# All of the program in the scheduler's table: keys, loads and weight conversion included, with other tile sizes, ranks and engine shares

## The chip, the cores and the metric

The kernel runs on one core of one Trainium2 chip. The metric is the device time of one launch, in microseconds (us), from the runs' own clock; a profile of one execution stands beside it.

## The reference, cut to what matters

Agent attention over 12480 tokens of width 128, and two feed-forward layers of width 2048 on its output, one after the other:

```python
def sm(a, b):
    s = scale * (a @ b.transpose(0, 2, 1))
    s = s - s.max(-1, keepdims=True)
    e = np.exp(s)
    return e / (e.sum(-1, keepdims=True) + 1e-09)
agent_v = sm(agents, k) @ v            # 49 agents over all keys
x = sm(q, agents) @ agent_v            # each token over 49 agents
h = x @ w_in                           # layer 1
P = a[0] + a[1]*h + a[2]*h**2 + a[3]*h**3
Q = 1.0 + abs(b[0])*abs(h) + abs(b[1])*h**2
x = (P / (Q + 1e-6)) @ w_out
r = np.maximum(x @ w2_in, 0.0)         # layer 2
out = (s * (r * r) + b) @ w2_out
```

All arrays are float32 except the four weight matrices. These come as float64, as pairs of 32-bit words, and the kernel makes float32 of them itself.

## The kernel before, in words

**Keys first.** The softmax over the keys needs all keys, so the kernel starts with 13 blocks of keys and values (`BLOCKS`: 12 of 1024 rows, one of 192). For a block `load_kv` loads keys and values on the SP queue, `keys_scores` (PE) multiplies agents and keys, `keys_max` (DVE) takes the running maximum, `keys_exp` (ACT) the exponentials, `keys_trans` and `keys_av` (PE) multiply them with the values, `keys_sum` and `keys_acc` (DVE) carry sum and product over to the next block. `keys_fold` closes it, and a copy into `avt` (L539) is its last step. The order of this stage is written out by hand in a loop at the end of the kernel.

**Weights.** Each of the four matrices is converted in 4 pieces (`CONV`, numbers 0 to 15: `w_in`, `w_out`, `w2_in`, `w2_out`). One piece is a load, two ACT passes (`conv_act`), four DVE passes (`conv_bit`: L390, L391, L393, L395) and a product and a sum on POOL (`conv_pool`: L407, L409). Pieces 0 to 9, and most of 10, stand between the steps of the key blocks in the same loop; the others come later, from the scheduler. Pieces of `w2_in` are also split into a high and a low part (`conv_hi`, `conv_lo`).

**The product of the agents' values and `w_in`** (`avw_mm`, `avw_hi`, `avw_lo`) is formed after `avt`, so that layer 1 of a token tile needs only its 49 softmax weights.

**Token tiles.** `TILES` cuts the tokens in 24 tiles of 512 and one of 192. A tile is worked on in units, 8 for a tile of 512: a unit is 1024 columns of hidden values. Layer 1 of unit p is the chain: `m1_h` on PE (L681, four matmuls), `m1_z` and `m1_abs` on ACT, `m1_u2` and `m1_u3` on DVE (L702, L705), `m1_w` on POOL (L696, L698), `m1_ln` and `m1_exp` on ACT, `m1_e`, `m1_m` and `m1_g` on DVE (L717, L721, L732), `m1_out` on PE (L740). The PSUM buffer that `m1_h` writes has one bank that all units share (`mid`), so `m1_h` of the next unit waits for `m1_u3` of this one. In the units of `ADD_POOL` the step `m1_g` isn't done by DVE but as two steps on POOL, `m1_a` (L725) and `m1_ga` (L729). After the last unit of a tile `m1_hi` and `m1_lo` (L751, writes `xl`) hand its result to layer 2: `m2_h` on PE (L763 to L765, into the one bank `bb`), `m2_relu` on ACT, the square on ACT or on POOL (L774, by `SQ_ACT`), `m2_out` on PE (L778). Layer 2 runs about one tile behind layer 1, so that both fill the same stretch of time.

**What sets the order.** `main_jobs` lists the steps of everything behind the keys with an engine, an estimated duration, predecessors, the buffers they use and a rank (unit number plus `RANK` of their kind). `in_order` places them one by one: the engine that can start first takes the job of lowest rank among those that are ready. `SLOTS` says how many buffers a kind has. The result is one fixed order on each engine:

```python
soon = max(free[e], min(at[k] for k in ks)) + 1e-9 + PATIENCE[e]
k = min((k for k in ks if at[k] <= soon), key=lambda k: jobs[k]["rank"])
```

Every engine works through its list in this order; a step that waits holds up all that stand behind it. All big transfers are issued on SP's queue. L326 is the one line that issues every ACT operation.

## Time and profile before

| | |
|---|---|
| time, median of 3 runs | 1355.6 us (1351.86 to 1356.43) |
| the profiled execution's own time | 1355.32 us |
| its span, first to last instruction | 1353.5 us |
| PE busy | 1259.5 us (93%) |
| DVE busy | 1228.9 us (91%) |
| ACT busy | 1178.3 us (87%) |
| POOL busy | 1122.5 us (83%) |
| mean granted PE clock | 0.974 |

The shares are means over stages with very different limits: a start in which no engine is full, some 1100 us in which tiles follow each other with the same pattern, and an end. The span leaves out 1.8 us of the execution's time.

### The profile page before, as it was taken

The numbers are of one execution on the slowest core, as the hardware profiler recorded it, in microseconds if no ns is written. First come the engines' busy times: TensorE is split into PE (matmuls) and PEld (weight loads), VectorE is DVE, ScalarE is ACT, GpSimd is POOL, SyncE is SP. The second block draws the span as 40 slices with busy tenths as digits, with TensorE's granted clock in tenths as the row PEclk, the third lists the DMA queues.
The fourth block names the chain that finished last, engine by engine and source line by source line (L and its number), as shares of the span: only waits on it lengthen the run. The fifth ranks groups of instructions, "written<-read, shape, count | busy, mean of one in ns | idle before, by whom it ended". The sixth has DMA issues, their size and how long they took to land.

```text
span 1353.5 us, 12969 instructions
## 1 busy us (share of the span) xinstructions
PE 1259.5 (93%) x4213; PEld 718.9 (53%) x4213; DVE 1228.9 (91%) x1178; ACT 1178.3 (87%) x1524; POOL 1122.5 (83%) x701
## 2 busy tenths in 40 slices
PE   5565699999999999999999999999999999999998
PEld 3342355555555555555555555555555555555565
DVE  5879989999999999999999999999999999999980
...
DMA packets 14005, 34.81 MB, mean 26 GB/s; under 512 B 2193, under 2 KB 2673, under 8 KB 13937
## 3 DMA queue, kind: packets, MB, share of 16 engines
...
q10 hardware_dynamic: 576, 0.00, 0.0%
...
## 4 chain that ended last, share of the span: by engine, by line
PE 61%; DVE 14%; POOL 11%; ACT 9%; issue 4%; DMA 1%; SPq 0%; ACTq 0%; DVEq 0%; POOLq 0%
PE acc L740 19%; PE acc L778 15%; PE xb L681 9%; PE bb L763 5%; PE bb L764 5%; PE bb L765 5%; POOL w_all L698 4%; POOL g_all L729 4%; DVE z_all L702 4%; DVE u_all L705 3%; ACT t_all L326 3%; POOL w_all L696 2%; DVE g_all L717 2%; ACT v_all L326 2%; DVE rb L721 2%
## 5 line engine op out<-in xcount | busy, mean ns | idle before, releaser
L698 POOL TENSOR_TENSOR w_all<-w_all,t_all 128x1024 f32<-128x1024 f32 (+1 forms) x196 | 464.3, 2369 | 18.6 <-ACT w_all L326 2.5
L740 PE MATMUL acc<-g_all,wout_sb 128*128 128x512 f32 (+1 forms) x800 | 374.2, 600 | 23.5 <-POOL g_all L729 11.8
L778 PE MATMUL acc<-v_all,w2out_sb 128*128 128x512 f32 (+1 forms) x800 | 379.3, 582 | 0.2 <-ACT o L326 0.2
L696 POOL TENSOR_SCALAR w_all<-t_all,absb 128x1024 f32<-128x1024 f32 (+1 forms) x193 | 232.4, 1204 | 111.1 <-ACT t_all L326 111.0
L326 ACT ACTIVATE v_all<-bb 128x512 f32<-128x512 f32 (+1 forms) x392 | 235.2, 600 | 45.8 <-PE bb L765 37.6
L702 DVE TENSOR_TENSOR z_all<-xb,z_all 128x1024 f32<-128x1024 f32 (+1 forms) x196 | 238.4, 1216 | 37.6 <-ACT z_all L326 35.8
L763 PE MATMUL bb<-xh,w2l 128*128 128x512 f32 (+1 forms) x400 | 251.6, 629 | 8.4 <-ACT v_all L326 7.7
L705 DVE SCALAR_TENSOR_TENSOR u_all<-z_all,prm,xb 128x1024 f32<-128x1024 f32 (+1 forms) x196 | 249.9, 1275 | 9.9
L326 ACT ACTIVATE t_all<-xb 128x1024 f32<-128x1024 f32 (+1 forms) x196 | 200.1, 1021 | 59.8 <-PE xb L681 59.1
L740 PEld LDWEIGHTS acc<-g_all,wout_sb 128*128 128x128 f32 x800 | 148.2, 193 | 181.2 <-issue 113.6
L717 DVE SCALAR_TENSOR_TENSOR g_all<-w_all,rb 128x1024 f32<-128x1024 f32 (+1 forms) x196 | 236.9, 1209 | 2.6 <-ACT rb L326 2.6
L326 ACT ACTIVATE z_all<-xb,prm 128x1024 f32<-128x1024 f32 (+1 forms) x196 | 236.6, 1207 | 0.0
L326 ACT ACTIVATE l_all<-w_all 128x1024 f32<-128x1024 f32 (+1 forms) x196 | 205.9, 1065 | 9.0 <-POOL w_all L698 7.1
L326 ACT ACTIVATE rb<-l_all 128x1024 f32<-128x1024 f32 (+1 forms) x196 | 204.3, 1042 | 3.5 <-DVE g_all L732 3.5
L774 POOL TENSOR_TENSOR v_all<-v_all 128x1024 f32<-128x1024 f32 x96 | 182.3, 1899 | 22.9 <-ACT v_all L326 22.9
L732 DVE SCALAR_TENSOR_TENSOR g_all<-u_all,prm,rb 128x1024 f32<-128x1024 f32 (+1 forms) x151 | 192.3, 1274 | 5.2
L778 PEld LDWEIGHTS acc<-v_all,w2out_sb 128*128 128x128 f32 x800 | 149.4, 189 | 78.2 <-issue 55.7
L721 DVE SCALAR_TENSOR_TENSOR rb<-g_all,rb 128x1024 f32<-128x1024 f32 (+1 forms) x151 | 184.2, 1220 | 3.5
L681 PE MATMUL xb<-pt,avwh 128*128 128x512 f32 (+1 forms) x400 | 167.7, 421 | 20.9 <-DVE u_all L705 15.5
L681 PE MATMUL xb<-pt,avwl 128*128 128x512 f32 (+1 forms) x400 | 157.9, 396 | 0.0
L764 PE MATMUL bb<-xh,w2h 128*128 128x512 f32 (+1 forms) x400 | 156.7, 392 | 0.0
L765 PE MATMUL bb<-xl,w2h 128*128 128x512 f32 (+1 forms) x400 | 155.4, 388 | 0.0
...
## 6 DMA issues: line engine op xcount, KB each, us to landing
...
```

Source lines behind the costliest of these rows:

```text
L326: return nc.scalar.activation(out=out, in_=in_, func=func, **kw)
L681: on_banks(nc.tensor.matmul(out=dst, lhsT=w[:, c * P:(c + 1) * P], rhs=pts[OF_UNIT[p][0]], start=first, stop=not first), {x}, "pe")
L696: nc.gpsimd.tensor_scalar(out=w, in0=t, scalar1=absb[:, 1:2], scalar2=absb[:, 0:1], op0=ALU.mult, op1=ALU.add)
L698: nc.gpsimd.tensor_tensor(out=w, in0=w, in1=t, op=ALU.mult)
L702: on_banks(nc.vector.tensor_tensor(out=z, in0=h_view(p), in1=z, op=ALU.mult), banks(p), "dve")
L705: on_banks(nc.vector.scalar_tensor_tensor(out=view("u", p), in0=view("z", p), scalar=a1, in1=h_view(p), op0=ALU.add, op1=ALU.mult), banks( ...
L717: nc.vector.scalar_tensor_tensor(out=view("g", p), in0=view("w", p), scalar=C1, in1=r_view(p), op0=ALU.add, op1=ALU.mult)
L740: nc.tensor.matmul(out=acc1[i][:, :n], lhsT=wout_sb[:, c * D:(c + 1) * D], rhs=g[:, at_(p, k), o:o + n], start=(c == 0), stop=(c == NCH - 1))
L763: nc.tensor.matmul(out=dst, lhsT=w2l[:, ws], rhs=xh, start=True, stop=False)
L764: nc.tensor.matmul(out=dst, lhsT=w2h[:, ws], rhs=xh, start=False, stop=False)
L765: nc.tensor.matmul(out=dst, lhsT=w2h[:, ws], rhs=xl, start=False, stop=True)
L778: nc.tensor.matmul(out=accs[1][:, :n], lhsT=w2out_sb[:, c * D:(c + 1) * D], rhs=m2_view(p)[:, k, o:o + n], start=(c == 0), stop=(c == NCH ...
```

## The change

What it does, part by part:

- **Tiles**: the first has 256 tokens (4 units) and the last 448 (8 units), with 23 of 512 between them. There are 196 units as before.
- **Order of the start**: key blocks, their loads, the conversion, the agent softmax of the first tile and the constants' loads become jobs of `start_jobs`, and `in_order` orders them with all others. The hand-written loop is gone. Loads of pieces 4 and up follow the last key block's load. Key blocks have 7 buffer pairs (in `l_all`, `g_all`, `u_all`) where they had 4.
- **Fewer operations on DVE in a key block**: the running maximum and its scaling are one TENSOR_SCALAR (before TENSOR_TENSOR and TENSOR_SCALAR); the running sum is a TENSOR_SCALAR (before SCALAR_TENSOR_TENSOR).
- **Conversion**: `conv_pool` becomes `conv_mul` (POOL) and `conv_add`, on DVE for pieces 0 to 9 and on POOL for the others; the clamp of pieces 4 to 15 goes from DVE to POOL.
- **Shares**: `ADD_POOL` has 3 units in 8 (before 2), `SQ_ACT` 5 in 8 (before 4), `W_ACT` units 4 to 11.
- **Buffers**: `z`, `t` 3 (before 2), `v` 5 (before 3).
- **Ranks** and planner constants are all others.
- Three matmuls on zeros stand ahead of the first key block; the four small constants are loaded on SP's queue and no more on ACT's.

```diff
-TILES = [512] * 24 + [192]
+TILES = [256] + [512] * 23 + [448]
...
-ADD_POOL = {p for p in range(12, NU - 4) if p % 8 in (1, 5)}
-SQ_ACT = {p for p, (_, j) in enumerate(OF_UNIT) if j in (0, 2, 4, 6) or p > NU - 5}
+W_ACT = {4, 5, 6, 7, 8, 9, 10, 11}
+ADD_POOL = {p for p in range(12, NU - 4) if p % 8 in (1, 4, 6)}
+SQ_ACT = {p for p, (_, j) in enumerate(OF_UNIT) if j in (1, 2, 4, 5, 7) or p > NU - 5}
...
+RANK = dict(h=-4.37, z=-5.75, abs=-0.66, y=-4.61, w=-1.15, u2=-4.49, u3=1.0, ln=7.57, exp=4.25, e=4.12,
...
+KV_TAG = "lgu"
...
+def start_jobs(add):
+
+    for i in range(2):
+        add(("load_q", i), "sp", 0.65, -58 + 30 * i, "key", (), [("qt", i)], -400)
+    last = NB - 1
+    for t, n in enumerate(BLOCKS):
+        o, at, part = KEY * t - 60, t - 300, n / 1024
+        kv = [(KV_TAG[t % 3], "kv", t, y) for y in range(2)]
...
+        add(("load_kv", t), "sp", 2.65 * part, o - AHEAD * KEY, "key", (), kv, at)
+        add(("keys_scores", t), "pe", 1.02, o, "key", [("load_kv", t)], kv + [sp], at)
+        add(("keys_max", t), "dve", 0.9, o, "key", [("keys_scores", t)] + prior, [sp], at)
...
+        add(("conv_load", n), "sp", 1.35, o - 8, "conv", [("load_kv", NB - 1)] if n >= 4 else [], raw, at)
...
+            clamp = n >= CLAMP and k == 0
+            add(("conv_bit", n, k), *(("pool", 0.65) if clamp else ("dve", us)), o, "conv",
+                [("conv_bit", n, k - 1) if k else ("conv_act", n)], raw + cv + tmp, at, True)
+        add(("conv_mul", n), "pool", 1.28, o, "conv", [("conv_bit", n, 3)], raw + cv + tmp, at)
+        add(("conv_add", n), *(("dve", 0.6) if n < DVE_ADDS else ("pool", 1.28)), o, "conv",
+            [("conv_mul", n)], raw + cv + tmp, at, True)
...
         if t:
-            nc.vector.tensor_tensor(out=m, in0=m, in1=cf[:, 0:1] if t == NB - 1 else ms[t - 1],
-                                    op=ALU.max)
-        nc.vector.tensor_scalar(out=nms[t], in0=m, scalar1=-SCALE, scalar2=None, op0=ALU.mult)
+            nc.vector.tensor_scalar(out=nms[t], in0=m, scalar1=-SCALE, op0=ALU.mult, op1=ALU.min,
+                                    scalar2=cf[:, 0:1] if t == NB - 1 else nms[t - 1])
+        else:
+            nc.vector.tensor_scalar(out=nms[t], in0=m, scalar1=-SCALE, scalar2=None, op0=ALU.mult)
...
-            nc.vector.scalar_tensor_tensor(out=ssum, in0=ssum, scalar=fs[t], in1=rss.pop(t),
-                                           op0=ALU.mult, op1=ALU.add)
+            nc.vector.tensor_scalar(out=ssum, in0=ssum, scalar1=fs[t], scalar2=rss.pop(t), op0=ALU.mult,
+                                    op1=ALU.add)
...
+        nc.vector.memset(win_sb[:, :512], 0.0)
...
+        for _ in range(3):
+            nc.tensor.matmul(out=bb_, lhsT=win_sb[:, :P], rhs=win_sb[:, :512], start=True, stop=True)
...
-        conv_load(0)
-        load_q(0)
-        load_kv(2)
-        conv_load(1)
-        load_q(1)
-        keys_scores(0)
...
```

**The loads at the start.** SP's queue, from the first load on. Before (`l_all` and `g_all` hold key blocks, `v_all` and `z_all` raw words of weights, `qt` queries, `agp` the agents):

```order
L812 DMA agp<-in_agents_dram 128x49
L448 DMA l_all<-in_k_dram 128x1024
L450 DMA l_all<-in_v_dram 128x1024
L448 DMA g_all<-in_k_dram 128x1024
L450 DMA g_all<-in_v_dram 128x1024
L372 DMA v_all<-in_moe_w_in_dram 128x1024
L594 DMA qt_131<-in_q_dram 128x512
L448 DMA l_all<-in_k_dram 128x1024
L450 DMA l_all<-in_v_dram 128x1024
L372 DMA z_all<-in_moe_w_in_dram 128x1024
```

And with the change, the same place (`u_all` holds key blocks too):

```order
L502 DMA l_all<-in_k_dram 128x1024
L504 DMA agp<-in_agents_dram 128x49
L506 DMA l_all<-in_v_dram 128x1024
L502 DMA g_all<-in_k_dram 128x1024
L506 DMA g_all<-in_v_dram 128x1024
L659 DMA qt_131<-in_q_dram 128x256
L502 DMA u_all<-in_k_dram 128x1024
L506 DMA u_all<-in_v_dram 128x1024
L502 DMA l_all<-in_k_dram 128x1024
L506 DMA l_all<-in_v_dram 128x1024
L424 DMA v_all<-in_moe_w_in_dram 128x1024
```

Four key blocks now stand ahead of the first piece of weights, where two stood.

**DVE after the keys.** Before, from the copy into `avt` to the first unit of layer 1 (`avwl` is the low part of the agents' product with `w_in`):

```order
L539 COPY avt<-bb 128x128
L390 TENSOR_SCALAR w_all<-w_all 128x512
L391 TENSOR_SCALAR w_all<-w_all 128x512
L393 SCALAR_TENSOR_TENSOR w_all<-v_all,w_all 128x512
L553 SCALAR_TENSOR_TENSOR avwl<-acc_79,cf,avwh 128x256
L553 SCALAR_TENSOR_TENSOR avwl<-acc_78,cf,avwh 128x256
L395 TENSOR_SCALAR t_all<-w_all 128x512
L617 TENSOR_REDUCE mx_657<-ss_102 128x4
L553 SCALAR_TENSOR_TENSOR avwl<-rb,cf,avwh 128x512 x2
L553 SCALAR_TENSOR_TENSOR avwl<-acc_79,cf,avwh 128x512
L702 TENSOR_TENSOR z_all<-xb,z_all 128x1024
```

With the change (L467 is `conv_add`, L449, L451 and L453 are conversion, L619 is `avw_lo`), the same place in part:

```order
L605 COPY avt<-bb 128x128
L467 TENSOR_TENSOR wout_sb<-u_all 128x512
L467 TENSOR_TENSOR wout_sb<-w_all 128x512
L619 SCALAR_TENSOR_TENSOR avwl<-acc_79,cf,avwh 128x256
L619 SCALAR_TENSOR_TENSOR avwl<-acc_78,cf,avwh 128x256
L453 TENSOR_SCALAR t_all<-w_all 128x512
L449 TENSOR_SCALAR w_all<-w_all 128x512
L682 TENSOR_REDUCE mx_623<-ss_102 128x4
L451 SCALAR_TENSOR_TENSOR w_all<-v_all,w_all 128x512
L467 TENSOR_TENSOR wout_sb<-u_all 128x512
```

Conversion that stood among the key blocks now stands here. From behind the copy into `avt` to the second L816 (`xl` of the second tile) the changed list has 30 operations of conversion, 15 each of `m1_u2` and `m1_u3`, and 13, 12 and 12 of `m1_e`, `m1_m` and `m1_g`. The list before, from the same copy to the second L751, has 24 of conversion, 19 each of `m1_u2` and `m1_u3`, and 17, 17 and 15 of the other three.

**DVE in a steady tile.** Before, around the hand-over to layer 2 (L702, L705 are `m1_u2`, `m1_u3`; L717, L721, L732 are `m1_e`, `m1_m`, `m1_g`; L617 is of the agent softmax):

```order
L702 TENSOR_TENSOR z_all<-xb,z_all 128x1024
L705 SCALAR_TENSOR_TENSOR u_all<-z_all,prm,xb 128x1024
L717 SCALAR_TENSOR_TENSOR g_all<-w_all,rb 128x1024
L751 TENSOR_TENSOR xl_3487<-acc_78,xh_3475 128x512
L721 SCALAR_TENSOR_TENSOR rb<-g_all,rb 128x1024
L732 SCALAR_TENSOR_TENSOR g_all<-u_all,prm,rb 128x1024
L702 TENSOR_TENSOR z_all<-xb,z_all 128x1024
```

With the change, the same place (L767, L770, L782, L786, L797 are the same five steps):

```order
L767 TENSOR_TENSOR z_all<-xb,z_all 128x1024
L770 SCALAR_TENSOR_TENSOR u_all<-z_all,prm,xb 128x1024
L782 SCALAR_TENSOR_TENSOR g_all<-w_all,rb 128x1024
L816 TENSOR_TENSOR xl_3685<-acc_78,xh_3677 128x512
L786 SCALAR_TENSOR_TENSOR g_all<-g_all,rb 128x1024
L767 TENSOR_TENSOR z_all<-xb,z_all 128x1024
L770 SCALAR_TENSOR_TENSOR u_all<-z_all,prm,xb 128x1024
```

The fifth step, `m1_g`, is missing in the interval that holds the hand-over. In a whole tile three of the eight intervals between one `m1_u2` and the next lack it, and two of these hold the hand-over and the `mx` row. Before, two lack it; one of them holds the `mx` row, and the hand-over stands in an interval of all five steps.

## Rows read from the trace of the kernel before

**Rows 1.** Windows: length, busy PE, PEld, DVE, ACT, POOL, clock, DMA, GB/s

```profile
10.00:75.20 65.20, 42.86 (x317) 25.40 (x315) 49.27 (x112) 32.79 (x78) 25.78 (x23) 0.86 0.75 286
75.20:162.90 87.70, 52.29 (x123) 28.59 (x124) 76.75 (x86) 57.83 (x73) 69.34 (x49) 0.73 0.09 27
162.90:217.30 54.40, 50.52 (x159) 28.84 (x158) 49.27 (x42) 48.46 (x61) 40.15 (x23) 0.97 0.01 2
266.30:315.70 49.40, 48.64 (x157) 27.62 (x157) 47.40 (x44) 46.12 (x59) 44.53 (x27) 1.00 0.03 11
```

**Rows 2.** Timeline of DVE: start, length, line, out<-in; stage ends

```profile
74.88 0.28 DVE L539 COPY avt<-bb 128x128 f32<-128x128 f32 x1
...
162.86 0.69 DVE L751 TENSOR_TENSOR xl<-acc,xh 128x512 fp32r<-128x512 f32 x1 [0.92 <-ACT xh L326]
...
217.29 0.68 DVE L751 TENSOR_TENSOR xl<-acc,xh 128x512 fp32r<-128x512 f32 x1
...
1301.96 0.69 DVE L751 TENSOR_TENSOR xl<-acc,xh 128x512 fp32r<-128x512 f32 x1
```

**Rows 3.** Timeline of PE and DVE inside one steady tile

```profile
622.00 1.02 PE L778 MATMUL acc<-v_all,w2out_sb 128*128 128x512 f32 x2
...
622.85 0.50 PE L763 MATMUL bb<-xh,w2l 128*128 128x512 f32 x1
...
633.28 1.22 DVE L702 TENSOR_TENSOR z_all<-xb,z_all 128x1024 f32<-128x1024 f32 x1
...
639.52 1.22 DVE L702 TENSOR_TENSOR z_all<-xb,z_all 128x1024 f32<-128x1024 f32 x1
...
642.28 0.47 PE L681 MATMUL xb<-pt,avwh 128*128 128x512 f32 x1 [0.18 <-DVE u_all L705]
...
645.23 1.23 DVE L702 TENSOR_TENSOR z_all<-xb,z_all 128x1024 f32<-128x1024 f32 x1 [0.70 <-ACT z_all L326]
...
648.18 0.39 PE L681 MATMUL xb<-pt,avwh 128*128 128x512 f32 x1
...
649.10 0.60 PE L658 MATMUL bb<-ident,pp 128*128 128x128 f32 x4
```

**Rows 4.** Windows of the keys' loads; last column GB/s

```profile
0.00:10.00 10.00, 1.66 (x4) 0.32 (x4) 1.79 (x6) 1.49 (x2) 2.15 (x11) 1.00 0.49 179
30.00:40.00 10.00, 5.36 (x50) 2.91 (x48) 9.51 (x20) 5.05 (x13) 5.23 (x5) 1.00 1.03 408
```

**Rows 5.** Timeline of PE, scores of the last full key block

```profile
62.62 1.08 PE L459 MATMUL xb<-g_all,agp 128*64 128x512 f32 x4
```

**Rows 6.** Groups of DVE instructions, first 75.2 us: count | busy, mean ns

```profile
L511 DVE SCALAR_TENSOR_TENSOR ssum<-ssum,f,rs 128x1 f32<-128x1 f32 x12 | 10.8, 904 | 1.0 <-ACT f L326 1.0
```

**Rows 7.** Timeline, DVE beside POOL

```profile
23.68 1.28 POOL L409 TENSOR_TENSOR win_sb<-w_all 128x512 f32<-128x512 f32 x1
...
23.71 1.25 DVE L511 SCALAR_TENSOR_TENSOR ssum<-ssum,f,rs 128x1 f32<-128x1 f32 x1
...
75.05 1.27 POOL L407 TENSOR_TENSOR u_all<-u_all,t_all 128x512 f32<-128x512 f32 x1 [2.45 <-DVE t_all L395]
...
75.08 1.51 DVE L390 TENSOR_SCALAR w_all<-w_all 128x512 f32<-128x512 f32 x1
```

**Rows 8.** Groups of DVE instructions, 100 to 163 us

```profile
L393 DVE SCALAR_TENSOR_TENSOR win_sb<-v_all,win_sb 128x512 int32<-128x512 int32 x3 | 4.5, 1499 | 0.0
...
L395 DVE TENSOR_SCALAR v_all<-win_sb 128x512 int32<-128x512 int32 x3 | 1.4, 465 | 0.0
```

**Rows 9.** Groups of POOL and ACT instructions, 600 to 800 us

```profile
L725 POOL TENSOR_SCALAR u_all<-u_all,one,prm 128x1024 f32<-128x1024 f32 x8 | 9.7, 1208 | 0.0
...
L729 POOL TENSOR_TENSOR g_all<-g_all,u_all 128x1024 f32<-128x1024 f32 x9 | 21.6, 2395 | 0.0
...
L774 POOL TENSOR_TENSOR v_all<-v_all 128x1024 f32<-128x1024 f32 x16 | 30.4, 1900 | 0.0
...
L326 ACT ACTIVATE v_all<-v_all 128x1024 f32<-128x1024 f32 x16 | 17.2, 1074 | 0.0
```

More of the change, by code (lines that the diff above doesn't have):

```diff
@@ L97, in add @@
         n = len(jobs)
+        if engine == "pe":
+            us *= slowed(key, unit)
         jobs[key] = dict(engine=engine, us=us, rank=(unit + RANK[kind], n), after=list(after),
@@ L177, in main_jobs @@
             if p in ADD_POOL:
-                add(("m1_a", p), "pool", w * 0.00117 + 0.07, p, "a", [("m1_u3", p)], [u])
+                add(("m1_a", p), "pool", w * 0.00117, p, "a", [("m1_u3", p)], [u])
                 add(("m1_ga", p), "pool", w * 0.00233, p, "ga", [("m1_m", p), ("m1_a", p)], [g, u])
@@ L183, in main_jobs @@
                 prior = [("m1_out", p, 0)] if k else [("m1_out", p - 1, 1)] if j else []
+                cs = range(0 if i else (2 * j + k + 1) * cpb)
                 add(("m1_out", p, k), "pe", pe_us(4, w / 2, cpb), p + 1, "out",
-                    [("m1_ga" if p in ADD_POOL else "m1_g", p)] + prior,
-                    [g, ("acc0", i)])
+                    [("m1_ga" if p in ADD_POOL else "m1_g", p)] + prior
+                    + [("conv_add", 4 + c // 4) for c in cs], [g, ("acc0", i)])
         end = f + UNITS[i] - 1
@@ L206, in main_jobs @@
                 add(("m2_out", p, k), "pe", pe_us(4, w / 2, cpb), behind, "m2out",
-                    [sq] + [("conv_pool", 12 + c // 4) for c in cs] + prior, [v, ("acc1", i)])
+                    [sq] + [("conv_add", 12 + c // 4) for c in cs] + prior, [v, ("acc1", i)])
             behind += 1
@@ L252, in in_order @@
         order.append(key)
-        slow = 1.5 if engine == "pe" and start < COLD else 1
+        slow = 1
         free[engine] = end = start + slow * jobs[key]["us"]
@@ L397, in conv_dve, with conv_mul, conv_add @@
         ]
-    def conv_bits(n):
-        for op in conv_dve(n):
-            op()
-    def conv_pool(n):
+    def conv_mul(n):
+        _, lf, s = cvs[n]
+        nc.gpsimd.tensor_tensor(out=lf, in0=lf, in1=s, op=ALU.mult)
+    def conv_add(n):
         name, _, u = CONV[n]
-        b, lf, s = cvs[n]
+        b, lf, _ = cvs[n]
         sl = slice(u * CW, (u + 1) * CW)
-        nc.gpsimd.tensor_tensor(out=lf, in0=lf, in1=s, op=ALU.mult)
         dst = {"in": win_sb, "out": wout_sb, "2out": w2out_sb}.get(name)
-        nc.gpsimd.tensor_tensor(out=b if dst is None else dst[:, sl], in0=lf, in1=b, op=ALU.add)
+        engine = nc.vector if n < DVE_ADDS else nc.gpsimd
+        engine.tensor_tensor(out=b if dst is None else dst[:, sl], in0=lf, in1=b, op=ALU.add)
     def conv_bit(n, k):
```

294 lines of the change are left out of this document (128 added, 166 removed).

## Prediction

> **What bounds the kernel now.** I read the windows of each stage first. The reader is to see four stages that are limited by different things [rows 1]. From 10 to 75 us, the keys, PE is busy 43 of 65 us and DVE 49. From 75 to 163 us, the first tile of layer 1, PE is busy 52 of 88 us at a granted clock of 0.73, so its work there is worth less than it looks; DVE is busy 77. From 163 us on PE is nearly full, and in a steady tile it is busy 48.6 of 49.4 us, DVE 47.4, ACT 46.1, POOL 44.5. The timeline of DVE dates the borders: the copy into `avt` ends at 75.2 us, `xl` of the first tile starts at 162.9, of the second at 217.3, of the twenty-fourth at 1302.0, which makes 49.3 us for a tile [rows 2].
>
> In the steady tile PE looks like the bound, but is not quite. Its own work, from the distance between starts, is 0.85 us for a matmul of an output (622.00 to 622.85) [rows 3], 0.92 for the four of `m1_h` (648.18 to 649.10) [rows 3], so 0.69 for the three of `m2_h`, and 0.6 for the transposes; with 0.9 for the agent scores, 32 x 0.85 + 8 x 0.92 + 16 x 0.69 + 1.5 = 47.1 us. So 2.2 us of each tile are waits. DVE sets them, together with one chain: from one `m1_u2` to the next DVE takes 6.24 us with all five steps (633.28 to 639.52). Where `m1_g` is POOL's, four steps would take 5.0, but the next `m1_u2` comes after 5.71 (639.52 to 645.23), the last 0.70 waiting for `m1_z`: `m1_u2` and `m1_u3` release the shared bank, PE fills it (642.28, after a wait), ACT reads it twice, DVE goes on [rows 3]. Six intervals of five steps, two of that chain, and about 1.0 for the hand-over and the agent softmax: 6 x 6.24 + 2 x 5.71 + 1.0 = 49.9, against 49.3 measured. The account is 0.5 too high, but says where the time is.
>
> **The keys' stage.** The change lets loads run ahead: seven buffer pairs, and only four pieces of weights ahead of the last key block. Twelve full blocks are 12.6 MB, the four pieces 2.1, queries 0.4: 15.1 MB. The first 10 us moved 1.8 MB (179 GB/s), full streaming is 408 GB/s [rows 4], so the last lands at 10 + 13.3/0.408 = 43 us. Then the closing chain: from the scores of the last full block at 62.62 [rows 5] to the end of the copy at 75.2 [rows 2] it took 12.5 us. I take `avt` at 43 + 12.5 = 55 us. DVE is not later: it had 49.3 us of work there [rows 1], and loses up to 12 x (0.9 - 0.2) = 8 us if the running sum, at 904 ns for one column [rows 6], no longer waits, and a quarter of the conversion. Bounds: 50 if the closing chain shrinks to 7 with conversion out of its way; 62 if POOL's products hold DVE as before. The three matmuls on zeros and the constants' loads on SP cost nothing: PE has no keys yet, and the small loads stand among block loads of 2.6 us each (1.05 MB at 408 GB/s).
>
> **POOL beside DVE.** The running sum that started 0.03 us after a POOL product of 1.28 us took 1.25 us; but a TENSOR_SCALAR of 512 columns that started 0.03 us after one of 1.27 took 1.51 [rows 7]. So the new form may wait as well; a row for one column beside POOL there is not. I give the new form no gain of its own, since the loads are later. The sum that `conv_add` makes on DVE has no row either; the nearest with two inputs in SBUF is L393, at 1.5 us each in the second stage, against 0.47 for L395 [rows 8].
> The Trainium skill, page "SBUF — State Buffer", section "Who interferes with whom", says that VectorE with two SBUF inputs or in a two-port mode, which it lists for tensor_scalar, and GpSimd exclude each other for a whole instruction. By that rule the new running sum would gain nothing and the five sums behind `avt` would wait; the trace agrees for the forms it has, 1.25 and 1.51 us.
>
> **From `avt` to the second tile's `xl`.** DVE's work decides: 76.75 + 49.27 = 126.0 us busy in 87.7 + 54.4 = 142.1 [rows 1], 89%. The changed list has 8 fewer of `m1_u2` and `m1_u3`, and 4, 5 and 3 fewer of `m1_e`, `m1_m`, `m1_g`: 20 at a fifth of 6.24 are 25.0 us less. It has 6 more of conversion, at 0.47 to 1.5; I take 0.6, since few of them are of the waiting kind, so 3.6 more. That leaves 104.6 us, at the same 89% 118. `xl` of the second tile: 55 + 118 = 173 us. Bounds: 50 + 104.6/0.95 = 160, and 62 + 124 = 186, with the six and the five sums at 1.5.
> At this point 12 units of layer 1 are done, before it was 16 at 217.3. Four units more at the steady 49.3/8 are 24.6: 198 against 217, **19 us gained**. Behind it PE has layer 2 of the short tile and layer 1 of the next to do; it isn't full there, and needn't be, since DVE sets the pace.
>
> **The steady tiles.** `m1_g` leaves DVE in a third interval, where the chain takes over; the hand-over and the `mx` row now lie in intervals that waited anyway. 5 x 6.24 + 3 x 5.71 + 0.4 = 48.7 against 49.9: 1.1 us less for a tile. The other engines get closer to it: ACT one more square of 1.07, so 47.2; POOL one more addition and product less one square, 44.5 + 1.21 + 2.40 - 1.90 = 46.2 [rows 1, 9]. At a tile of 48.2 us ACT would be 98% busy, and what it does in order (`m1_z` and `m1_abs` behind squares and logarithms) will come late now and then. I take 0.8 us. Bounds: 0, if that eats all, and 1.3; PE's own 47.1 allows no more than 2.2. From the sixteenth unit on there are 180 units, 22.5 tiles: **18 us gained**.
>
> **The end.** Behind the last `m1_out` the list before has 9 `m2_h` and 14 `m2_out` of 512 columns and 8 of each of 384; the changed one 16 of each of 448 and 4 `m2_out` of 512. At 0.69 and 0.85 that is 27.4 and 25.0 us: **2 us gained**, give or take 2.
>
> **Sum.** 1353.5 - 19 - 18 - 2 = 1314.5 of span; with the 1.8 us around it 1316.3 for an execution like the profiled one, whose 1355.3 is the median of the runs (1355.6) but for 0.3. I say 1316.
>
> **The rivals.**
> *The steady tile stays at 49.3.* For it: ACT and POOL have lists of 47.2 and 46.2 us and no slack to absorb each other. Against: every engine still has 2 us a tile left. 1316 + 18 = 1334.
> *The stalls only move.* The running sum keeps its 0.7 us in 12 blocks and the five DVE sums cost 0.9 more each: 8 + 4.5, 1328. For it: both waiting forms [rows 7]. Against: in the keys' stage the loads are later. This is also what the rule of the Trainium skill's page "SBUF — State Buffer" (section "Who interferes with whom") gives.
> *The keys' stage is bound otherwise*, by PE at its lower clock (mean 0.86 there now [rows 1]) or by buffers that come free late: `avt` at 70, 1331.
> *All of it goes better*: `avt` at 50, DVE 95% busy behind it, 1.3 us a tile: 1316 - 5 - 8 - 11 = 1292.
> *Slower.* POOL's list puts a `m1_a` or `m1_ga` directly ahead of `m1_w`. If each of the three additions a tile delays `m1_w` by its 1.21 us, the logarithm waits, in ACT's order the relu behind it waits, and with the one bank `bb` PE: 3.6 us against the 2.2 of waits there are, so 1.4 a tile more, 22.5 x 1.4 = 32, less 21 of start and end: 1355 + 11 = 1366. It decides from 21/22.5 = 0.93 us a tile on, a tile of 50.2. Against it: `t` has three buffers, so POOL may run late by a unit.
>
> **How the numbers follow.** Forecast 0.52, with 1303 to 1327 as its own range from the bounds of its terms; steady tile unchanged 0.18; stalls move 0.10; better 0.10; keys otherwise 0.05; slower 0.05. From 1296 to 1338 leaves out about 0.06 below and 0.10 above. Under 0.3%, 4 us, a difference can't be told from none here. All cases but the last lie over 4 us below 1355.6: faster 0.93, same 0.02, slower 0.05.
>
> **What would show it.** The copy into `avt` at 50 to 60 us, with loads at some 400 GB/s until about 43; `xl` of the second tile at 165 to 181; starts of `xl` 48.2 to 48.9 apart from then on, DVE busy 46 to 47 of it, ACT near 47; intervals of four steps on DVE at 5.7 with the hand-over inside. The prediction fails if `xl`s are 49.3 or more apart, or if DVE, behind `avt`, waits for POOL's `m1_w` or for conversion.

## The result, and the profile after

The changed kernel takes 1336.4 us (median of 4 runs, 1334.5 to 1338.2) where the kernel before takes 1354.0 beside it: a ratio of 0.987, 95% interval 0.984 to 0.990. The time lies inside the range of the prediction (1296 to 1338), but the gain is 17.6 us where 39.6 were forecast (1355.6 to 1316).

The windows of the changed kernel by stage, in the columns of [rows 1]:

```profile
10.00:66.26 56.26, 38.01 (x305) 23.76 (x303) 35.10 (x89) 29.77 (x74) 19.10 (x15) 0.80 0.76 286
66.26:83.74 17.48, 10.02 (x30) 6.52 (x30) 13.14 (x20) 9.63 (x17) 13.75 (x10) 0.70 0.39 136
83.74:171.49 87.75, 57.41 (x202) 40.43 (x202) 78.97 (x80) 69.06 (x82) 74.79 (x49) 0.73 0.06 18
188.41:240.79 52.38, 47.84 (x147) 27.80 (x146) 46.19 (x42) 47.06 (x60) 45.47 (x28) 0.92 0.03 8
581.54:630.21 48.67, 48.54 (x158) 27.29 (x157) 46.10 (x42) 47.23 (x60) 46.34 (x29) 1.00 0.04 11
```

The borders, from the timeline of DVE (the copy into `avt`, the first and the thirteenth `m1_u2`, `xl` of the first, second, third and last full tile):

```profile
65.98 0.28 DVE L605 COPY avt<-bb 128x128 f32<-128x128 f32 x1
83.74 1.21 DVE L767 TENSOR_TENSOR z_all<-xb,z_all 128x1024 f32<-128x1024 f32 x1
137.69 0.41 DVE L816 TENSOR_TENSOR xl<-acc,xh 128x256 fp32r<-128x256 f32 x1
171.49 1.23 DVE L767 TENSOR_TENSOR z_all<-xb,z_all 128x1024 f32<-128x1024 f32 x1
188.41 0.69 DVE L816 TENSOR_TENSOR xl<-acc,xh 128x512 fp32r<-128x512 f32 x1 [0.92 <-ACT xh L383]
240.79 0.69 DVE L816 TENSOR_TENSOR xl<-acc,xh 128x512 fp32r<-128x512 f32 x1
1263.31 0.68 DVE L816 TENSOR_TENSOR xl<-acc,xh 128x512 fp32r<-128x512 f32 x1
```

These rows are to be laid beside [rows 1, 2] by units done, since the tiles are cut differently. At 240.8 us the changed kernel has done 20 units. The kernel before has 16 at 217.3 and 24 at 266.3, so 20 at 241.8: **the whole start has gained 1.0 us**. At 1263.3 it has done 188, the kernel before at 1277.9 (midway between its last two full tiles): 14.6, so the steady tiles gained 13.6. The spans end 17.1 apart (1353.5 and 1336.4), so the end gained 2.5. Steady tile and end came nearly as forecast (18, of 22.5 tiles where these are 21, and 2); of the 19 us of the start one came.

Two further profiles of the same kernel (below) have `avt` at 64.1 and 64.4 and the third `xl` at 238.8 and 239.5, so the start's gain is 1 to 3 us, whichever profile is taken.

### The profile page after: what moved, and what is told of

Its sections match the earlier page's. It is cut to its first block, busy times and chain, and to the rows that moved or that the text cites. A ratio compares the mean times of both kernels' runs of the same rounds, so it can differ in the third digit from the quotient of the medians.

```text
span 1336.4 us, 13092 instructions
## 1 busy us (share of the span) xinstructions
PE 1262.7 (94%) x4219; PEld 719.7 (54%) x4219; DVE 1193.9 (89%) x1142; ACT 1209.0 (90%) x1552; POOL 1168.4 (87%) x721
## 4 chain that ended last, share of the span: by engine, by line
PE 72%; ACT 17%; DVE 4%; issue 3%; DMA 2%; POOL 1%; SPq 0%; ACTq 0%; DVEq 0%
PE acc L805 21%; PE acc L843 17%; PE xb L746 10%; PE bb L828 8%; PE bb L829 6%; PE bb L830 6%; ACT z_all L383 4%; ACT v_all L383 3%; ACT l_all L383 3%; ACT t_all L383 3%; PE bb L665 2%; ACT rb L383 2%; ACT xh L383 1%; PE acc L565 1%; DMA g_all<-in_k_dram 1%
## 5 line engine op out<-in xcount | busy, mean ns | idle before, releaser
L805 PE MATMUL acc<-g_all,wout_sb 128*128 128x512 f32 (+2 forms) x800 | 387.4, 598 | 13.8 <-DVE g_all L797 13.8
L843 PE MATMUL acc<-v_all,w2out_sb 128*128 128x512 f32 (+2 forms) x800 | 375.8, 581 | 0.1
L767 DVE TENSOR_TENSOR z_all<-xb,z_all 128x1024 f32<-128x1024 f32 (+1 forms) x196 | 238.2, 1215 | 50.0 <-ACT t_all L383 49.9
L770 DVE SCALAR_TENSOR_TENSOR u_all<-z_all,prm,xb 128x1024 f32<-128x1024 f32 (+1 forms) x196 | 249.7, 1274 | 5.9
L782 DVE SCALAR_TENSOR_TENSOR g_all<-w_all,rb 128x1024 f32<-128x1024 f32 (+1 forms) x196 | 237.2, 1210 | 7.1 <-ACT rb L383 3.2
L805 PEld LDWEIGHTS acc<-g_all,wout_sb 128*128 128x128 f32 x800 | 152.9, 196 | 123.2 <-issue 68.8
L828 PE MATMUL bb<-xh,w2l 128*128 128x512 f32 (+2 forms) x400 | 201.7, 504 | 10.1 <-ACT v_all L383 7.4
L746 PE MATMUL xb<-pt,avwh 128*128 128x512 f32 (+2 forms) x400 | 194.2, 486 | 12.4 <-DVE u_all L770 12.3
L794 POOL TENSOR_TENSOR g_all<-g_all,u_all 128x1024 f32<-128x1024 f32 (+1 forms) x68 | 161.0, 2368 | 41.1 <-DVE g_all L786 20.3
L828 PEld LDWEIGHTS bb<-xh,w2l 128*128 128x128 f32 x400 | 75.6, 189 | 187.0 <-ACT v_all L383 162.7
L797 DVE SCALAR_TENSOR_TENSOR g_all<-u_all,prm,rb 128x1024 f32<-128x1024 f32 (+1 forms) x128 | 163.1, 1275 | 4.4
L746 PE MATMUL xb<-pt,avwl 128*128 128x512 f32 (+2 forms) x400 | 159.2, 398 | 1.5 <-DVE avwl L619 1.5
L786 DVE SCALAR_TENSOR_TENSOR rb<-g_all,rb 128x1024 f32<-128x1024 f32 (+1 forms) x128 | 156.4, 1222 | 3.5
L839 POOL TENSOR_TENSOR v_all<-v_all 128x1024 f32<-128x1024 f32 (+1 forms) x73 | 138.1, 1892 | 24.0 <-ACT v_all L383 24.0
## 6 DMA issues: line engine op xcount, KB each, us to landing
l_all<-in_v_dram SPq DMA_DIRECT2D x4, 512.0 KB, 10.1
```

Of the source, the lines that this page charges most:

```text
L746: on_banks(nc.tensor.matmul(out=dst, lhsT=w[:, c * P:(c + 1) * P], rhs=pts[OF_UNIT[p][0]], start=first, stop=not first), {x}, "pe")
L767: on_banks(nc.vector.tensor_tensor(out=z, in0=h_view(p), in1=z, op=ALU.mult), banks(p), "dve")
L770: on_banks(nc.vector.scalar_tensor_tensor(out=view("u", p), in0=view("z", p), scalar=a1, in1=h_view(p), op0=ALU.add, op1=ALU.mult), banks( ...
L782: nc.vector.scalar_tensor_tensor(out=view("g", p), in0=view("w", p), scalar=C1, in1=r_view(p), op0=ALU.add, op1=ALU.mult)
L794: nc.gpsimd.tensor_tensor(out=view("g", p), in0=view("g", p), in1=view("u", p), op=ALU.mult)
L797: nc.vector.scalar_tensor_tensor(out=view("g", p), in0=view("u", p), scalar=a0, in1=r_view(p), op0=ALU.add, op1=ALU.mult)
```

## The experiments

Three questions: what held up the start, what makes the steady tile 48.7 us, and whether the keys' smaller edits count. Times are medians beside runs of the kernel before on the same chip (1353.8 to 1354.7).

**Without the conversion of three matrices.**

```diff
-    for n in range(16):
+    for n in range(4):
         o, at = (WIN0 + WINS * n if n < 4 else CONV0 + CONVS * n), n - 290
...
```

> The changed kernel without the loads and the conversion of pieces 4 to 15 (the matrices w_out, w2_in and w2_out are filled with a constant, so the output means nothing; pieces 0 to 3 stay). If conversion that stands in the lists of ACT, DVE and POOL ahead of the keys' closing steps and of the agents' product is what ate the gain at the start: the last keys still land at about 47 us, the closing chain shrinks from 18.5 to about 12.5, the copy into avt comes at 58 to 60 instead of 66.0, the first m1_u2 within 12 us of it (70 to 72 instead of 83.7), the thirteenth m1_u2 at 150 or earlier instead of 171.5, and the time is 1310 to 1318. If the chain of the start itself is the limit (latency from step to step, PE at its lower clock), conversion only fills gaps: avt at 64, the first m1_u2 at 80, the thirteenth at 167 or later, time 1332.

1357.1 us, no faster than before (ratio 1.002, 1.001 to 1.003), though a large part of the work is gone. Its start is near what the first account expected: `avt` at 58.6, the first `m1_u2` at 72.1, the thirteenth at 152.9, 3 us later than it gave. But from there on the tiles are 50.0, 50.7 and 51.4 us apart, in turn. The planner, given fewer steps at the start, wrote another order for all the rest. So a run with a new plan tells of two things at once; the start is read at the thirteenth `m1_u2`, and the steady tile apart from it.

**The same, with the lists kept.** No new plan: the steps are struck out of the lists of the change.

```diff
         for name, *args in order:
-            run[name](*args)
+            if not (name.startswith("conv_") and args[0] >= 4):
+                run[name](*args)
...
```

> The changed kernel with its lists kept word for word, and only the loads and the conversion of pieces 4 to 15 struck out of them (the three matrices are filled with a constant, so the output means nothing). In the run without conversion the planner had also written another order for all later tiles, and these were 50.7 us apart. If the order decides the steady tile: tiles 48.6 to 48.7 apart here, the thirteenth m1_u2 at 151 to 155 (as in that run, 152.9), and the time 1316 to 1320. If the slower tiles come from the faster start itself (buffers or queues in another state), they are 50 or more apart again and the time is 1345 or more.

1316.3 us (ratio 0.972, 0.970 to 0.975), tiles 48.7 apart. Its borders, from the timeline of DVE:

```profile
56.83 0.29 DVE L605 COPY avt<-bb 128x128 f32<-128x128 f32 x1 [0.65 <-PE bb L602]
65.10 1.22 DVE L767 TENSOR_TENSOR z_all<-xb,z_all 128x1024 f32<-128x1024 f32 x1 [0.29 <-ACT t_all L383]
147.03 1.22 DVE L767 TENSOR_TENSOR z_all<-xb,z_all 128x1024 f32<-128x1024 f32 x1
215.08 0.68 DVE L816 TENSOR_TENSOR xl<-acc,xh 128x512 fp32r<-128x512 f32 x1
```

So twelve pieces of conversion cost the start 24.5 us by the thirteenth `m1_u2` (171.5 to 147.0): 9.2 ahead of `avt`, 9.5 between it and the first `m1_u2` (17.5 us to 8.0), 5.8 in the next twelve units (87.8 to 81.9). Against the two later profiles of the change (thirteenth at 169.7 and 170.1) it is 23. The thirteenth came 4 us earlier than expected. `avt` at 56.8 and a time of 1316 are what the prediction gave for the kernel that does this work; in the time this is partly luck, for the second `xl` comes at 162.9 here and not at 173.

**Only the last two matrices left out.** As above, with `args[0] >= 8`.

> The changed kernel's lists with the loads and the conversion of pieces 8 to 15 struck out (w2_in and w2_out are filled with a constant, so the output means nothing), pieces 4 to 7 kept. Striking out 4 to 15 gave avt at 56.8, the first m1_u2 at 65.1 and the thirteenth at 147.0. If pieces 4 to 7 in front of the keys' closing steps cost what was lost there: avt stays at 61 to 63; the first m1_u2 at 70 to 73, since pieces 8 to 10 stood between avt and it; the thirteenth at 153 to 156; time 1321 to 1325. If the later pieces only fill gaps: first m1_u2 at 78 or later, thirteenth at 163 or later, time 1330 or more.

1323.9 us. `avt` at 64.1, first `m1_u2` at 76.1, thirteenth at 157.8. `avt` stands where the change's later profiles have it (64.1 and 64.4), so what delays it is pieces 4 to 7. Of the 12 to 13 us won, 6 lie between `avt` and the first `m1_u2`: pieces that no unit needs before layer 2 begins stood ahead of it. The first `m1_u2` came 3 us later than expected, `avt` 1 and the thirteenth 2.

**Other places for the same work.** The planner is told that loads take longer, as the trace shows.

```diff
-        add(("load_kv", t), "sp", 2.65 * part, ...
+        add(("load_kv", t), "sp", 3.2 * part, ...
-        add(("conv_load", n), "sp", 1.35, ...
+        add(("conv_load", n), "sp", 2.2, ...
```

> The changed kernel, but its planner is told that loads take longer (3.2 us for a key block, was 2.65; 2.2 for a piece of weights, was 1.35), as the trace shows them. Work is the same; only places in the lists change: conv_act of piece 10 moves behind the first m1_z, the conversion of two pieces moves behind the last keys' steps. If it is the place of these steps that costs: avt at 61 to 63 (66.0), first m1_u2 at 75 to 78 (83.7), thirteenth at 165 to 168 (171.5), time 1330 to 1332. If conversion is work owed that must be done before layer 1 can go on, the first m1_u2 may come earlier, but the thirteenth stays at 170 to 172 and the time at 1335 to 1338.

1340.1 us (ratio 0.990, 0.988 to 0.991). `avt` comes at 61.9, but the first `m1_u2` at 81.1 and the thirteenth at 174.6. The first account holds for `avt` alone; what was moved out of its way is paid behind it, by 2 us more than the second account gave.

**Weights' loads between the key blocks again** (`n >= 4` in `conv_load`'s condition becomes `n >= 10`, ranks of pieces 0 to 9 at -56.2 + 2.7 n, planner's loads 2.9 and 2.2 us), and one piece only (`n >= 5`).

> The changed kernel with the loads of pieces 0 to 9 between the key blocks, about as before (planner: 2.9 us for a block's load, 2.2 for a piece's; the order of the steady tiles stays that of the change). If conversion is work owed that DVE and POOL must do before layer 1 can run, on either side of the keys: avt at 68 to 74, the first m1_u2 6 to 10 us behind it instead of 18, the thirteenth at 166 to 172 as in the changed kernel, time 1332 to 1337. If keys first is what wins: thirteenth at 174 or later, 1340 or more. If keys first is what loses: thirteenth at 162 or earlier, 1328 or less.

> The same with one more piece, the fifth, ahead of the last key blocks' loads, and with the planner's longer durations for loads, which put the pieces' loads between the blocks earlier. Owed work: avt at 63 to 66, thirteenth m1_u2 at 166 to 172, 1332 to 1337. Otherwise as for the run with ten, with half its size or less.

1338.0 and 1337.6 us, up to 1 us over what owed work gave. With ten pieces between the blocks `avt` comes at 68.7, the first `m1_u2` 14.5 us behind it (6 to 10 were expected), the thirteenth at 171.8. With five: 62.7, 15.7 us, 171.7. The loads' order moves `avt` by 6 us and the thirteenth unit by nothing: conversion is owed on one side of the keys or the other.

**Which engine owes it.** Two runs move conversion-time work from POOL: the first part of `m1_w` in units 0 to 3 to ACT (`W_ACT` from 0 on), and the sums of pieces 10 to 15 to DVE (`DVE_ADDS = 16`).

> The changed kernel with the first part of m1_w on ACT in units 0 to 11 (before: 4 to 11): 4 x 1.2 us move from POOL to ACT in the first four units. Steady order unchanged. If POOL, with conversion's clamps, products and splits, is what holds up the first units: thirteenth m1_u2 at 166 to 169 instead of 171.5, time 1331 to 1333. If DVE or the chain from step to step is: no change (171 to 173), 1335 to 1338, or up to 2 us later since ACT's list gets longer.

> The changed kernel with the closing sum of pieces 10 to 15 on DVE too (six steps of 1.3 us less on POOL, six of 0.7 to 1.1 more on DVE). Steady order unchanged. Taking 1.2 us a unit off POOL in the first four units didn't help, so if DVE is what the first units wait for: thirteenth m1_u2 1 to 4 us later than in the changed kernel, time 1336 to 1340. If POOL's conversion is: 2 to 6 us earlier, time 1330 to 1334.

1339.6 (ratio 0.989, 0.987 to 0.991) and 1346.4 us (0.994, 0.992 to 0.995). The thirteenth `m1_u2` comes at 172.8 and at 175.0: POOL relieved at the cost of ACT or of DVE brings nothing, and six more sums on DVE cost 10 us of time, more than twice what was expected. So in the first units DVE is short, and POOL is not what holds them up; that ACT comes next behind DVE is argued, not shown.

**The constants' loads** (`nc.sync.dma_start` in `params` becomes `nc.scalar.dma_start`) and **the keys' old DVE forms** (TENSOR_TENSOR and TENSOR_SCALAR for the maximum, SCALAR_TENSOR_TENSOR for the sum).

> The changed kernel with the four loads of small constants issued on ACT's queue, as before, and not on SP's between the key blocks. The prediction priced them at nothing. In the trace of the change SP issued them at 8.7 to 11.7 us, 1.3 us apart, each after an earlier load had landed, and the chip read 298 GB/s from 10 to 20 us where it read 402 before. If they held up the block loads: 400 GB/s from 10 to 20 us, scores of the fifth block at 18 to 20 us instead of 22.65, last block 2 to 3 us earlier, avt at 63 to 64. If those slots don't matter: fifth block at 22 to 23, avt at 66. The time changes in either case by no more than 3 us, since conversion is owed behind avt (1333 to 1337).

> The changed kernel with the keys' DVE steps in the form of before: running maximum by two operations, running sum by SCALAR_TENSOR_TENSOR. Lists stay as they are. If the old forms wait for POOL whenever it runs (904 and 488 ns in the trace before, 267 and nothing in the change): 12 x 0.6 + 11 x 0.5, 13 us more of DVE work before avt, of which DVE's idle time (38 of 66 us busy) hides most: avt at 66 to 68, time 1336 to 1339. If these waits come only with POOL's products, which are now four in the first 50 us: the running sum takes 210 to 400 ns, avt at 66, time 1335 to 1337.

1335.0 and 1334.5 us, both within the runs of the change. With the constants on ACT's queue 330 GB/s were read from 10 to 20 us (298 in the change), and the fifth block's scores start at 21.4; in the other runs of changed kernels, which have them on SP's, they start at 21.0 to 23.0, so the 22.65 of the first profile isn't shown to be the constants' doing. `avt` comes at 62.3, earlier than both accounts gave, and a little earlier than in nine profiles with the same order up to there, or nearly the same (62.7 to 66.0): these differ among themselves by more. The old forms mostly take as little time as the new ones (283 ns a sum, new 267), for POOL now runs only four products in the first 50 us. Beside one of them the two differ. First the pair of the run with the old forms, then the pair of the change, POOL's product and DVE's running sum:

```profile
39.19 1.27 POOL L459 TENSOR_TENSOR w_all<-w_all,t_all 128x512 f32<-128x512 f32 x1 [5.93 <-DVE t_all L453]
39.44 1.05 DVE L573 SCALAR_TENSOR_TENSOR ssum<-ssum,f,rs 128x1 f32<-128x1 f32 x1 [0.39 <-ACT f L383]
```

```profile
39.00 1.27 POOL L459 TENSOR_TENSOR w_all<-w_all,t_all 128x512 f32<-128x512 f32 x1 [5.63 <-ACT e L383]
39.20 0.27 DVE L573 TENSOR_SCALAR ssum<-ssum,f,rs 128x1 f32<-128x1 f32 x1 [0.34 <-ACT f L383]
```

**The steady tile: shares, or the order?** The shares of before (`ADD_POOL` 1 and 5 of 8, `SQ_ACT` 0, 2, 4, 6); the tiles of before; one number of the planner (2.65 to 2.9 us for a key block's load).

> The changed kernel with the engine shares of before in the steady tiles: m1_g on POOL in 2 units of 8 instead of 3, squares on ACT in 4 of 8 instead of 5. Ranks, buffers, tiles and start stay those of the change. If the shares bring the 0.72 us a tile (48.65 against 49.37): tiles 49.2 to 49.5 apart, time 1350 to 1353. If buffers and ranks bring it: tiles at most 48.9 apart, time at most 1342. A tile between the two divides it.

> The changed kernel with the tiles of before (24 of 512 and one of 192). By the prediction's terms the end grows by 2 to 2.5 us and the start hardly changes: 1338 to 1340. Rival: the short first tile costs as much as it brings, because its layer 2 is over when layer 1 of the next tile is handed over and PE has nothing to fill the gap (the third xl of the changed kernel comes 52.4 us after the second); then the time is 1334 to 1336 at 2.4 us more for the end.

> The changed kernel with one number of the planner's changed: 2.9 us for the load of a key block, was 2.65. All work, shares, ranks and buffers stay, but the planner writes another order for all tiles: m1_e of a unit follows m1_u2 of the next unit but one in the change, of the next unit here. If the order decides the steady tile: tiles 50 to 51.4 apart (50.7 on the mean in the run without conversion that had such an order), time 1366 to 1385. If shares, ranks and buffers decide it: 48.7, time 1332 to 1338.

1371.1, 1371.5 and 1382.4 us, all slower than before (ratios 1.013, 1.013 and 1.021, 1.019 to 1.022), with tiles of 50.4, 50.4 and 50.7 us. The third has the same work, shares, ranks and buffers as the change: **the order alone is worth 2 us a tile, 46 us in all**. The first two were meant for something else (shares, end and short first tile) and don't answer it, as their plans fell into other orders too; what the shares bring as a whole, and what a short first tile brings, was not settled. One interval of DVE in a steady tile of the change, then of the run with 2.9 us:

```profile
584.13 1.22 DVE L767 TENSOR_TENSOR z_all<-xb,z_all 128x1024 f32<-128x1024 f32 x1 [0.78 <-ACT t_all L383]
585.39 1.28 DVE L770 SCALAR_TENSOR_TENSOR u_all<-z_all,prm,xb 128x1024 f32<-128x1024 f32 x1
586.59 1.21 DVE L782 SCALAR_TENSOR_TENSOR g_all<-w_all,rb 128x1024 f32<-128x1024 f32 x1
...
590.29 1.22 DVE L767 TENSOR_TENSOR z_all<-xb,z_all 128x1024 f32<-128x1024 f32 x1
...
595.94 1.23 DVE L767 TENSOR_TENSOR z_all<-xb,z_all 128x1024 f32<-128x1024 f32 x1 [0.46 <-ACT t_all L383]
```

```profile
600.09 1.28 DVE L770 SCALAR_TENSOR_TENSOR u_all<-z_all,prm,xb 128x1024 f32<-128x1024 f32 x1
601.97 1.22 DVE L782 SCALAR_TENSOR_TENSOR g_all<-w_all,rb 128x1024 f32<-128x1024 f32 x1 [0.60 <-ACT rb L383]
...
621.62 1.22 DVE L782 SCALAR_TENSOR_TENSOR g_all<-w_all,rb 128x1024 f32<-128x1024 f32 x1 [0.64 <-POOL w_all L763]
...
634.01 1.22 DVE L782 SCALAR_TENSOR_TENSOR g_all<-w_all,rb 128x1024 f32<-128x1024 f32 x1 [0.58 <-POOL w_all L761]
```

In the change `m1_e` (L782) belongs to the unit two behind the `m1_u2` that stands before it; its exponential is long done, and DVE waits only for `m1_abs`, in the short intervals. In the other order `m1_e` belongs to the unit one behind, and waits 0.4 to 0.6 us in four of eight intervals, for the exponential or, through it, for POOL's `m1_w`: 2.2 us a tile. Two behind is not enough by itself: the run with the old shares has it too, in another order of the rest, and its tiles take 50.4.

**One share undone, lists kept**: in the unit of each tile whose interval holds the hand-over, `m1_g` goes back to DVE.

```diff
+    DROP = {p for p in ADD_POOL if p % 8 == 4}
...
+            if args and args[0] in DROP and name in ("m1_a", "m1_ga"):
+                continue
             run[name](*args)
+            if name == "m1_m" and args[0] in DROP:
+                m1_g(*args)
```

> The changed kernel's lists, but in one unit of each tile (number mod 8 is 4, the one whose interval on DVE holds the hand-over) m1_g is done by DVE directly behind m1_m, and its two steps on POOL are struck out; all other rows stay. That gives DVE the five-step interval with the hand-over in it that the kernel before had. By the prediction's account of intervals on DVE a tile grows by 0.5 to 1.2 us: 49.2 to 49.8, time 1347 to 1361. If PE's own list sets the steady tile of the changed kernel (PE is busy 48.54 of 48.67 us, DVE 46.1), DVE has 2.5 us of slack for these 1.28 us: tiles at most 48.9 apart, time at most 1341.

1342.7 us (ratio 0.991, 0.990 to 0.993), tiles 49.0 apart. 1.28 us more on DVE cost 0.3 us a tile: between the two accounts, nearer to the one by PE. With the rest of the change in place, this third unit of `m1_g` on POOL is worth 0.3 of the 0.7 us that a tile gained.

**PE's clock.** Matmuls on 512 columns that nobody reads, in PE's idle times: two at 180 us, or these and eleven more from 77 to 130 us.

```diff
             run[name](*args)
+            for _ in range(FILL.get((name, *args), 0)):
+                nc.tensor.matmul(out=bb_, lhsT=wout_sb[:, :P], rhs=wout_sb[:, :512], start=True, stop=True)
```

> The changed kernel with two matmuls on 512 columns, whose result nobody reads, in the 2.45 us for which PE waits just before the second tile is handed over (at 180 us). In the profile of the run with the keys' old forms the clock stayed at 1.00 from there on, and the third tile took 49.4 us instead of 52.4. If the clock is the cause and this idle time lets it fall: clock 0.97 or more and at most 50.5 us in the third tile, second xl 1 to 2 us earlier, time 3 to 5 us less than the changed kernel's on the same chip. If the clock falls for other reasons: 52 us again and no difference.

> The same two and eleven more in PE's idle times from 77 to 130 us, where the clock was 0.50 to 0.69. If PE at half clock holds up the first units: thirteenth m1_u2 4 to 8 us earlier than in the changed kernel (170 to 171.5), time 6 to 10 less. If DVE, POOL and ACT with conversion hold them up: thirteenth at most 2 us earlier, and the time as with two matmuls.

> The changed kernel unchanged, beside the two on the same chip: 1334 to 1338, third tile 52.4 us at a clock of 0.92 (by the other account, some executions at 1.00).

1335.1, 1333.4 and 1335.9 us; the ratios, 0.986 (0.984 to 0.987), 0.985 (0.983 to 0.986) and 0.986 (0.985 to 0.987), don't part them. Windows of the run with two matmuls, and of the run with the keys' old forms, whose lists are those of the change:

```profile
180.00:190.00 10.00, 6.41 (x18) 2.68 (x16) 9.03 (x9) 8.55 (x11) 7.26 (x5) 1.00 0.01 2
200.00:210.00 10.00, 8.71 (x19) 5.26 (x20) 8.54 (x9) 7.48 (x12) 8.85 (x6) 0.66 0.04 13
```

```profile
184.76:234.20 49.44, 44.08 (x146) 24.71 (x145) 45.91 (x41) 46.93 (x60) 45.50 (x28) 1.00 0.03 8
```

The two matmuls did hold the clock at 1.00 from 180 to 190 us (0.66 to 0.83 in three profiles of the change), and the second `xl` came 0.9 us earlier than in the run beside it. But PE then waits for ACT's relu (1.95 us until 188.7, 1.54 until 200.6), the clock falls after 200, and the third tile takes 52.2 us as before. In the run with the old forms, where it didn't fall, the third tile took 49.4, and PE was busy 44.1 us of it, not 47.8. So 3 us of the third tile go with the clock. Why it didn't fall there stays open: PE's waits are much the same in that run (2.45 us until 180.4, 2.21 until 188.2, 1.54 until 200.1). With fillers at the start the clock from 64 to 180 us is 0.85 (0.74 to 0.76), but the thirteenth `m1_u2` comes only 2.0 us earlier, 1.0 of it already at `avt`: PE at half clock is not what holds up the first units. This version is the fastest that was run, by an amount that the runs can't tell from none.

**The changed kernel a second time.**

> The changed kernel unchanged, for a second profile: in four kernels with the same lists up to avt, or nearly so, avt came at 61.9 to 63.1, where the one profile of the changed kernel has 66.0. If that profile had late loads by chance: avt at 62 to 64, second xl at 184 to 186, time 1334 to 1336. If not: avt at 65 to 67.

1335.5 us; `avt` at 64.4, second `xl` at 187.0, both 1.5 us earlier than in the first profile and between the two accounts, and the time as before.

## Why the prediction was right or wrong, point by point

**Right in size, in mechanism only in part: the steady tile.** Forecast 0.8 us less, measured 49.37 to 48.67. The account of intervals on DVE gave 48.7: in the timeline above the five-step interval from 584.13 to 590.29 is 6.16 us, the four-step one with the `mx` row to 595.94 is 5.65, its last 0.46 us waiting for ACT; 6.24 and 5.71 were used. Busy times came as worked out: ACT 47.2, POOL 46.3, DVE 46.1 us. But the prediction put the whole gain down to the third unit whose `m1_g` leaves DVE, and that unit put back on DVE in the same lists cost 0.3 us, not 0.7 or more. Where the other 0.4 come from (the squares, the buffers, the order) stays open. Nor did it say that these shares give it only in some orders: other plans with the same shares, with `m1_e` one unit behind, take 50.4 to 50.7. Of the rivals, "steady unchanged" fell, and so did "slower" by POOL's additions ahead of `m1_w`.

**Wrong in it: PE's own 47.1 us.** The 0.69 us of an `m2_h` were taken from `m1_h` rows. Behind an output it takes 0.81, as this timeline of PE in the changed kernel shows (596.45 to 597.26):

```profile
596.45 0.50 PE L828 MATMUL bb<-xh,w2l 128*128 128x512 f32 x1
596.79 0.39 PE L829 MATMUL bb<-xh,w2h 128*128 128x512 f32 x1
597.02 0.40 PE L830 MATMUL bb<-xl,w2h 128*128 128x512 f32 x1
597.26 1.02 PE L843 MATMUL acc<-v_all,w2out_sb 128*128 128x512 f32 x2
```

With eleven of sixteen behind an output, 1.3 us more, PE's list is over 48 us; PE is busy 48.54 of 48.67. So PE's list allowed about 1 us of gain and not the 2.2 of the prediction. That PE and DVE now limit the tile together, and that one share undone costs only 0.3 for this reason, is argued from these numbers.

**Right: the end**, 2.5 us for a forecast of 2.

**Wrong, and the step that failed: the start, "55 + 118 = 173" and the 19 us that follow from it.** It has three parts, of 11.3, 4.2 and 3.1 us, which make up the 18 that are missing.

*"I take `avt` at 43 + 12.5 = 55"*: the copy ended at 66.3, in other executions at 64.4 and 64.7. What was loaded was not far off: by 20 us 5.7 MB had come (the forecast's 1.8 + 4.1), though spread otherwise, as two windows of the change show (last column GB/s):

```profile
0.00:10.00 10.00, 7.18 (x16) 2.46 (x17) 3.29 (x11) 2.06 (x3) 2.07 (x11) 1.00 0.80 268
10.00:20.00 10.00, 5.50 (x52) 3.23 (x50) 4.99 (x13) 4.63 (x12) 0.00 (x0) 0.97 0.85 298
```

But the scores of the last full block began at 47.78 and not at 43 (at 45.7 and 46.0 in the other two executions): 3 to 5 us of the 11. The larger part is the closing chain, taken over from before at 12.5 us: from these scores to the end of the copy (66.26) it took 18.5. With conversion struck out of the same lists it takes 10.7 (46.40 to 57.1). The timelines of PE (one line) and ACT in the changed kernel show why:

```profile
47.78 1.08 PE L518 MATMUL xb<-u_all,agp 128*64 128x512 f32 x4
...
50.60 1.21 ACT L383 ACTIVATE w_all<-v_all 128x512 f32<-128x512 f32 x2 [1.44 <-DMA v_all<-in_moe_w_out_dram]
51.70 0.68 ACT L383 ACTIVATE e<-xb,nm 128x512 f32<-128x512 f32 x1
...
56.08 0.60 ACT L383 ACTIVATE et<-bb 128x512 f32<-128x512 f32 x1 [0.89 <-PE bb L550]
56.58 1.23 ACT L383 ACTIVATE w_all<-v_all 128x512 f32<-128x512 f32 x2
57.71 1.21 ACT L383 ACTIVATE u_all<-v_all 128x512 f32<-128x512 f32 x2
...
60.70 1.24 ACT L383 ACTIVATE w_all<-v_all 128x512 f32<-128x512 f32 x2 [0.53 <-DVE wout_sb L467]
61.84 0.26 ACT L383 ACTIVATE et<-bb 96x128 f32<-96x128 f32 x1
```

The conversion of the fifth piece waits 1.44 us for its load, and the exponentials of the last full block, ready since 49.9, stand behind it; the last block's `et` stands behind another. On DVE the last sum of the product (`accx`), whose matmuls ended at 62.85, stands behind conversion (L453), and so does the copy (L451; it starts at 65.98):

```profile
62.67 1.38 DVE L453 TENSOR_SCALAR t_all<-w_all 128x512 int32<-128x512 int32 x1
...
64.31 0.33 DVE L581 SCALAR_TENSOR_TENSOR accx<-accx,f,acc 128x128 f32<-128x128 f32 x1
64.56 1.49 DVE L451 SCALAR_TENSOR_TENSOR u_all<-v_all,u_all 128x512 int32<-128x512 int32 x1
```

The bounds of 50 to 62 were too narrow: the lower one took conversion out of the way of this chain, the upper one added only what DVE might wait for POOL, and neither asked which steps of conversion the changed lists put into it.

*"It has 6 more of conversion ... so 3.6 more"*: here the form of the sum held, and this term was too small. DVE was busy 107.9 us from the copy to the second `xl`, which is 88% of 122.2 where 89% were taken; the forecast was 104.6. The 30 operations of conversion took 24.7 us, the 24 of before 16.9: 7.8 more, not 3.6. The prediction took few of them to be of the waiting kind; the window (columns of [rows 1]), and two of the groups in it (count, busy us, mean ns), show otherwise:

```profile
66.26:188.41 122.15, 81.21 (x271) 54.93 (x272) 107.86 (x113) 90.20 (x111) 101.60 (x66) 0.74 0.10 33
```

```profile
L451 DVE SCALAR_TENSOR_TENSOR win_sb<-v_all,win_sb 128x512 int32<-128x512 int32 x5 | 6.2, 1233 | 0.0
L449 DVE TENSOR_SCALAR win_sb<-win_sb 128x512 int32<-128x512 int32 x5 | 4.4, 873 | 0.9 <-POOL win_sb L446 0.9
```

The shortest of these took 0.68 and 0.43 us. The loss lies ahead of the first unit: from `avt` to the first `m1_u2` it took 17.5 us, where it had been 11.6 (75.2 to 86.7), and the twelve units behind it 87.8, where they had taken 88.0. The first and the thirteenth `m1_u2` before:

```profile
86.73 1.23 DVE L702 TENSOR_TENSOR z_all<-xb,z_all 128x1024 f32<-128x1024 f32 x1 [0.34 <-ACT z_all L326]
174.71 1.23 DVE L702 TENSOR_TENSOR z_all<-xb,z_all 128x1024 f32<-128x1024 f32 x1 [2.38 <-ACT z_all L326]
```

*"Four units more at the steady 49.3/8"*: the third tile took 52.4 us, 3.1 more, at a granted clock of 0.92; in the one profile of these lists with 1.00 it took 49.4.

The sums hide a simpler one. Twelve pieces of conversion cost 23 to 24.5 us of the start in the changed kernel, and to put their loads elsewhere gained nothing: at the thirteenth `m1_u2` the kernel before stands at 174.7, the change at 171.5, ten pieces between the key blocks at 171.8. Keys first brought `avt` 9 us forward, and the pieces that had been converted in those 9 us came due right behind it.

**The keys' smaller edits.** No gain for the new sum was right: DVE is busy only 35 of 56 us there, and POOL seldom stands beside it. The rival "stalls only move" rested on one column behaving as 512 do. It doesn't: the sum as TENSOR_SCALAR took 0.27 us with POOL's product under way. The rival's other half came true in size: 4.5 us for waits behind `avt`, and conversion there took 4.2 more than was priced, though less in the five sums (0.68 to 1.00 us each) than in the steps before them. The Trainium skill's page "SBUF — State Buffer", section "Who interferes with whom", lists tensor_scalar among the operations that can exclude POOL, when their operands meet conditions that the prediction left out; the row above shows that a TENSOR_SCALAR of one column didn't wait, and that a SCALAR_TENSOR_TENSOR with two inputs in SBUF did (1.05 us), as the page has it. Constants' loads at nothing and matmuls on zeros at nothing: the first held by the run on ACT's queue, the second was not tried alone.
